# Attention, two feed-forward layers and a layer norm on one core: the ordering model lets VectorE and GpSimd take turns in SBUF, and gets new durations for the products

## The chip, the cores and the metric

One core of a Trainium2 chip runs the whole program as one launch. The metric is the device time of one execution in microseconds (us), the median of several. TensorE (PE) multiplies, VectorE (DVE), ScalarE (ACT) and GpSimd (POOL) do the elementwise work, SyncE (SP) issues the transfers.

## The reference

`x` is the output of an attention whose keys and values are averaged over 8 positions; two feed-forward layers of width 2048 follow, the first with a low-rank mixing over the sequence, the second behind a layer norm. All arrays are fp32.

```python
k_p = k.reshape(B, H, Sp, pool, D).mean(axis=3)        # B 8, H 8, S 576, D 64, pool 8, Sp 72
v_p = v.reshape(B, H, Sp, pool, D).mean(axis=3)
scores = scale * np.matmul(q, k_p.transpose(0, 1, 3, 2))
attn = softmax(scores)
x = np.matmul(attn, v_p)                               # then [8, 576, 512]
u = x + (x.transpose(0, 2, 1) @ U @ V).transpose(0, 2, 1)      # rank 32
x = u + np.maximum(u @ w_ch1, 0.0) @ w_ch2                     # 512 -> 2048 -> 512
xn = (x - mean) / np.sqrt(var + 1e-06) * g_ln
out = x + np.maximum(xn @ w2_ch1, 0.0) @ w2_ch2                # 512 -> 2048 -> 512
```

## The kernel before, in words

Products keep fp32 accuracy by splitting each operand into a high and a low fp32r part (`split`: a rounded copy, then a subtraction) and multiplying high by high, high by low and low by high. The weights of the feed-forward layers come as 64-bit words and are decoded with integer operations on VectorE (`decode`).

**First phase** (`phase_a`, up to about 665 us): for each of 8 batches the attention (`att_prep` averages the keys, `att_prep_v` the values, `att_m` does the softmax, `att_vm` the low-rank mixing), and one batch later the first 8 of the 16 hidden blocks of the first layer (`a_l1`, `a_l2`) out of resident weights. Before the first batch can go through `a_l1`, its 16 half blocks of weights have to be decoded and split.

**Three passes** (`passes`): the 4608 rows stand in 9 groups of 512. Pass 0 does the other 8 hidden blocks of the first layer, passes 1 and 2 the second layer. A group of a pass has 4 units, a unit 2 hidden blocks; 108 units in all. In a unit (`unit`) the first product is done with seven 2x2-block products (p1 to p7) of 6 matmuls with 256 columns each, into the PSUM tiles `pa` and `pbc`; VectorE adds pieces (lines 1301 and 1307), ScalarE takes the relu and VectorE its low part (line 1271). The second product (`second`, line 1331) is done a unit later in 8 pieces of three matmuls with 512 columns, into four PSUM tiles `py`. At a group's end VectorE adds the four `py` to `res` (`finish`, line 1346), which frees them for the next group.

While pass 0 does group g, the layer norm of group g-1 runs beside it (`norm`), in two halves of 256 rows: sum over the channels (lines 1412 to 1414), its high and low part `lnh` and `lnl`, a pair of matmuls with `ones` for the mean (lines 1404 and 1405), subtraction (1428), squares and their sum (1436 to 1440), the pair of matmuls again for the variance, a reciprocal on VectorE (1452) with a refinement (1454 to 1460), and four scalings of `res` (1467). Also beside it run `group_prep` (loading the next group, three differences of blocks at line 1198, and seven splits into `op` tiles, lines 369, 371 and 494), `residual` (line 1383), and, near the change of a pass, `load_pair` (the next weights, line 1163 and splits).

**The order is made by a planner.** Each operation is recorded by `Order.op` with its possible engines, a cost for each, and its tiles. `Order.schedule` then plays the program through a model: engines, costs, ring slots, semaphore delays. At each step an engine takes the available operation with the lowest `prio`, unless `better` says that another engine would end it sooner. Which engine an operation goes to and the order on each engine come out of this model alone; on the chip each engine then runs its list in order and waits only for data.

In the model before, VectorE and GpSimd never hinder each other. A product with n columns costs max(107, n / 2.4 + 2) ns: 108.7 for 256, 215.3 for 512. `prio` is the running sum of these costs at the point where the operation was recorded, plus a bias. GpSimd's cost of a 512-element line is 1227 ns (`c_pool`), VectorE's 601 (`c_dve`) or 335 (`c_fast`, for copies and scalar operations).

Of the kernel before, what the change touches and what calls it, by code (L numbers as in the profile page):

```python
# [16 lines left out]
PSUM = bass.MemoryType.PSUM  # L17
# [28 lines left out]

class Ring:


# [32 lines left out]


class Op:
    __slots__ = ("engs", "fn", "preds", "succs", "bufs", "prio", "ready", "wait", "eng", "start", "end", "alloc", "size")


PE, ACT, DVE, GP, SY = "pe", "act", "dve", "pool", "sync"  # L90
# [10 lines left out]
class Order:  # L101
# [3 lines left out]
    def op(self, engs, fn, r=(), w=(), prio=None, size=0):  # L105
        o = Op()
        o.engs, o.fn, o.succs, o.size = engs, fn, [], size
        o.prio = (self.clk + self.bias) if prio is None else prio
        o.eng = o.end = o.start = None
        preds, bufs = set(), []  # L110
        for wr, lst in ((False, r), (True, w)):
            for x in lst:
                b, k = x if isinstance(x, tuple) else (x, None)
                if b not in bufs:
                    bufs.append(b)
                for k2, (lw, rd) in b.acc.items():
                    if k is None or k2 is None or k == k2:
                        if lw is not None:
                            preds.add(lw)
                        if wr:  # L120
                            preds.update(rd)
        for wr, lst in ((False, r), (True, w)):
            for x in lst:
                b, k = x if isinstance(x, tuple) else (x, None)
                if wr:
                    if k is None:
                        b.acc = {None: (o, [])}
                    else:
                        b.acc[k] = (o, [])
                else:  # L130
                    lw, rd = b.acc.get(k, (None, []))
                    b.acc[k] = (lw, rd + [o])
        preds.discard(o)
        o.preds = len(preds)
        for p in preds:
            p.succs.append(o)
        o.bufs = [b for b in bufs if b.ring is not None]
        for b in o.bufs:
            b.left += 1
            b.ring.pool.left += 1  # L140
        o.ready = {e: 0.0 for e in engs}
        self.ops.append(o)
        if PE in engs:
            self.clk += engs[PE]
        return o


    def schedule(self):
# [5 lines left out]
        look = {e: never for e in engines}  # L154
        events, parked, order = [], {}, []
        dma, n, left, warm = 0.0, 0, len(self.ops), 0.0

        def at(e, t):
            if t < look[e]:
                look[e] = t  # L160
                heapq.heappush(events, (t, e))
# [8 lines left out]
        def blocked(o, t):  # L170

            for b in o.bufs:
                if b.slot is None:
                    r = b.ring
                    for a in r.pool.after:
                        if a.left:
                            return a
                        if a.end > t:
                            return a.end
                    if r.fifo and b.seq != r.turn:  # L180
                        return r, b.seq
                    if not r.free:
                        return r, None
                    if r.free[0][0] > t:
                        return r.free[0][0]
            return None
# [18 lines left out]
        while left:  # L205
# [4 lines left out]
            t, e = heapq.heappop(events)  # L210
# [7 lines left out]
            while fut and fut[0][0] <= t:  # L218
                _, k, o = heapq.heappop(fut)
                if o.eng is None:  # L220
                    heapq.heappush(av, (o.prio, k, o))
            got, later = None, []
            while av:
                pr, k, o = heapq.heappop(av)
                if o.eng is not None:
                    continue
                if any(x != e and better(o, x, t, t + o.engs[e] - (EAGER if e == GP else 0)) for x in o.engs):
                    later.append((pr, k, o))
                    continue
                why = blocked(o, t)  # L230
                if why is None:
                    got = o
                    break
                if isinstance(why, float):
                    heapq.heappush(fut, (why, k, o))
                else:
                    parked.setdefault(why, []).append(o)
# [8 lines left out]
            o, idle = got, 0  # L246
# [5 lines left out]
            o.eng, o.start = e, t  # L252
            free[e] = t + cost
            o.end = free[e]
            if e == SY:
                dma = max(dma, t + 1300) + o.size / RATE
                o.end = dma + 1000
# [88 lines left out]


def c_pe(n, k=1):
    return k * max(107.0, n / 2.4 + 2)


class View:
# [21 lines left out]
class Kern:  # L374
# [754 lines left out]
    def load_pair(self, p, j):  # L1129
# [30 lines left out]
        def comb(dst, i, key, a, b, op, extra=()):  # L1160
            o.op(
                {GP: c_pool(256), DVE: c_dve(256)},
                lambda e: getattr(e, op)(dst.t[:, i * 256 : i * 256 + 256], a(), b()),
                r=[x, *extra],
                w=[(dst, i)],
            )
# [426 lines left out]
```

## Time and profile before

| | |
|---|---|
| median of three timed runs | 1886.73 us (1885.02 to 1887.83) |
| profiled execution | 1894.99 us, span 1893.2 us |
| PE busy | 1798.2 us, 95% of the span |
| DVE busy | 1343.4 us, 71% |
| ACT busy | 691.3 us, 37% |
| POOL busy | 649.4 us, 34% |
| mean granted TensorE clock | 0.976 |

The span runs from the first to the last instruction; the profiled execution has 1.8 us around it. Busy shares are means over stages that differ, so the stages have to be read one by one. A granted clock of 1.0 is 2.4 GHz, of 0.5 it is 1.2 GHz; a value in between is the mean over a stretch. A matmul's records overlap with the next one's, so a stretch in which PE is fully busy can still run at the slower clock.

### The profile page before, as it was taken

To read this page: it belongs to the slowest core of one execution; us is meant where nothing else is said; L and a number is where in the kernel's file an instruction comes from. 1 tells how busy PE (TensorE), PEld (TensorE's weight loads), DVE (VectorE), ACT (ScalarE), POOL (GpSimd) and SP (SyncE) were. 2 spreads that over 40 slices of the span, in tenths; PEclk is the share of its full clock that TensorE was granted. 3 is DMA by queue.
4 is the path that set the end of the run, shared out by engine and by line. 5 is a ranking of instruction groups with operands and counts; after the bars stand their busy time and mean duration, and the time that the engine had idled before them with its cause. 6 is when DMAs were issued, how large, how long until landed. Compare 5 with 4: busy or idle time off the path is not lost. (4 is left out here: it accounts for less than half of the span.)

```text
span 1893.2 us, 30247 instructions
## 1 busy us (share of the span) xinstructions
PE 1798.2 (95%) x11482; PEld 1631.2 (86%) x11482; DVE 1343.4 (71%) x2414; ACT 691.3 (37%) x1965; POOL 649.4 (34%) x656
## 2 busy tenths in 40 slices
PE   5789999999999989999999989999999999999999
PEld 4578999999999988888787868888889898999888
DVE  8998888988854677988888898667543764444543
ACT  4445555555554223323333343323222322222221
POOL 5563444444301244443444664111111442111210
PEclk9699999999999999999999999999999999999999
DMA  5534454444312251323333332433211342222211
GB/s 167 157 116 148 127 159 151 140 139 158 107 55 81 88 188 60 124 99 112 112 112 112 111 119 93 140 128 112 79 47 65 129 153 109 93 109 89 89 68 45
DMA packets 88642, 212.42 MB, mean 112 GB/s; under 512 B 9264, under 2 KB 17456, under 8 KB 82736
## 3 DMA queue, kind: packets, MB, share of 16 engines
q1 hardware_dynamic: 88352, 210.49, 33.7%
q8 instruction: 90, 1.47, 0.3%
q14 instruction: 56, 0.46, 0.1%
q10 hardware_dynamic: 144, 0.00, 0.0%
HBM read 141.25 MB, written 69.21 MB: 111 GB/s over the span
## 5 line engine op out<-in xcount | busy, mean ns | idle before, releaser
L1331 PE MATMUL py<-hid,w2h 128*128 128x512 f32 x1728 | 552.2, 401 | 11.6 <-DVE res L1346 10.5
L1243 PE MATMUL pa<-op,w1h 128*128 128x256 f32 x1728 | 334.3, 286 | 17.8 <-DVE pa L1307 11.7
L1243 PEld LDWEIGHTS pa<-op,w1h 128*128 128x128 f32 x1728 | 296.8, 193 | 59.2 <-DVE pa L1307 18.6
L1331 PE MATMUL py<-hid,w2l 128*128 128x512 f32 x864 | 339.8, 393 | 0.0
L1331 PEld LDWEIGHTS py<-hid,w2h 128*128 128x128 f32 x1728 | 282.7, 193 | 27.7 <-DVE res L1346 8.4
L1243 PE MATMUL pbc<-op,w1h 128*128 128x256 f32 x1296 | 248.0, 284 | 3.3 <-DVE hid L1271 3.3
L1243 PEld LDWEIGHTS pbc<-op,w1h 128*128 128x128 f32 x1296 | 222.3, 191 | 29.8 <-DVE hid L1271 3.5
L1243 PE MATMUL pa<-op,w1l 128*128 128x256 f32 x864 | 246.8, 286 | 0.0
L1013 PE MATMUL pa<-hid,wh 128*128 128x288 f32 x1024 | 216.8, 304 | 10.1 <-DVE op L1025 9.7
L1046 PE MATMUL pbc<-op,wh 128*128 128x288 f32 x1024 | 215.5, 302 | 1.0 <-DVE wh L371 1.0
L1301 DVE TENSOR_TENSOR pbc<-s,pbc 128x512 f32<-128x512 f32 x108 | 74.6, 691 | 189.2 <-PE pbc L1243 185.9
L1331 PEld LDWEIGHTS py<-hid,w2l 128*128 128x128 f32 x864 | 164.8, 191 | 37.2
L1243 PE MATMUL pbc<-op,w1l 128*128 128x256 f32 x648 | 184.3, 284 | 0.0
L1013 PEld LDWEIGHTS pa<-hid,wh 128*128 128x128 f32 x1024 | 164.4, 190 | 16.6 <-DVE op L1025 15.4
L1046 PEld LDWEIGHTS pbc<-op,wh 128*128 128x128 f32 x1024 | 163.8, 188 | 5.9 <-issue 2.8
L1243 PEld LDWEIGHTS pa<-op,w1l 128*128 128x128 f32 x864 | 166.4, 193 | 0.0
L1265 ACT ACTIVATE hid<-pbc 128x512 fp32r<-128x512 f32 x108 | 64.6, 598 | 273.4 <-DVE pbc L1301 273.2
L1046 PE MATMUL pbc<-op,wl 128*128 128x288 f32 x512 | 151.5, 296 | 1.4 <-DVE wl L494 1.4
L1013 PE MATMUL pa<-hid,wl 128*128 128x288 f32 x512 | 151.4, 296 | 0.0
L369 ACT COPY s<-pa 128x256 f32<-128x256 f32 x204 | 75.7, 372 | 169.9 <-PE pa L1243 165.2
L494 POOL TENSOR_TENSOR op<-t,op 128x512 fp32r<-128x512 f32 x32 | 44.6, 1393 | 256.8 <-DVE op L371 250.9
L1265 ACT ACTIVATE hid<-pa 128x512 fp32r<-128x512 f32 x108 | 64.6, 598 | 168.2 <-PE pa L1243 159.3
(191 smaller groups left out, 3370.6 us busy)
## 6 DMA issues: line engine op xcount, KB each, us to landing
xraw<-n_d SPq DMA_DIRECT2D x18, 1024.0 KB, 4.8
wraw<-wC SPq DMA_DIRECT2D x32, 512.0 KB, 3.8
wraw<-wA SPq DMA_DIRECT2D x24, 512.0 KB, 3.8
w_d<-wx SPq DMA_DIRECT2D x48, 256.0 KB, 4.0
wraw<-w_d SPq DMA_DIRECT2D x48, 256.0 KB, 3.9
k<-kT SPq DMA_DIRECT2D x32, 288.0 KB, 2.9
q<-qT SPq DMA_DIRECT2D x32, 288.0 KB, 3.0
v<-v SPq DMA_DIRECT2D x32, 288.0 KB
```

Of the source, the lines that this page charges most:

```text
L369: e.copy(dst, src)
L494: lambda e: e.tensor_sub(lo(), src(), hi().bitcast(F32)),
L1013: e.matmul(ps.t[:, :SH], w.t[:, c], u, start=(i == 0), stop=(i == 3 * NCC - 1))
L1046: e.matmul(ps.t[:, :SH], w.t[:, c], x, start=(f == 0 and j == 0), stop=(f == NA - 1 and j == 2))
L1243: e.matmul(bank.t[:, sl], w.t[:, self.WCOL[k], c], u.t[:, t], start=(first and i == 0), stop=(last and i == 5), skip_group_check=True,)
L1265: lambda e: e.activation(h.t[:, :TG], bank.t, AF.Relu),
L1301: o.op({DVE: c_dve(TG)}, lambda e: e.tensor_add(c.t, s.t, c.t), r=[s], w=[c])
L1331: e.matmul(y.t, w.t[:, i, c], x.t[:, :TG], start=(first and q == 0), stop=(last and q == 2))
```

## The change

The model gets a port that VectorE and GpSimd share. An operation none of whose tiles lies in PSUM is marked `port`. While one of the two engines runs such an operation in the model, the other may not start one; it notes what it asked for (`asked`), goes on to operations that don't need the port, and the engine that has had the port leaves it to the other's operation where that has the lower `prio`. Nothing is enforced on the chip: no wait is added, and the turns exist only in the model that makes the order. The mark takes in every operation of VectorE without a PSUM tile, reductions and reciprocals too.

The second edit sets a product with n columns to n / 2.3 + 5 ns: 116.3 for 256, 227.6 for 512. With it all `prio` grow by some 6 to 7%, while the biases stay.

```diff
-    __slots__ = (..., "alloc", "size")
+    __slots__ = (..., "alloc", "size", "port")
...
+        o.port = not any(b.ring.pool.space is PSUM for b in o.bufs)
...
+        port, other, asked = {DVE: 0.0, GP: 0.0}, {DVE: GP, GP: DVE}, {}
...
             got, later = None, []
+            asked.pop(e, None)
...
                 why = blocked(o, t)
+                if why is None and e in port and o.port:
+                    z = asked.get(other[e])
+                    if port[other[e]] > t:
+                        why = port[other[e]]
+                        asked.setdefault(e, o)
+                    elif z is not None and z.eng is None and z.prio < o.prio:
+                        why = t + 1.0
...
+            if e in port and o.port:
+                port[e] = o.end
...
-    return k * max(107.0, n / 2.4 + 2)
+    return k * max(107.0, n / 2.3 + 5)
```

In the whole program GpSimd's list falls from 658 to 448 instructions, VectorE's grows from 2416 to 2514 and ScalarE's from 1648 to 1730; TensorE's 11292 and SyncE's 544 are the same in number. The lines of the changed kernel are 14 higher in this part of the file (line 1467 before is 1481 now).

**GpSimd, pass 0, a middle group, from the refinement of the first half's reciprocal on** (`op` are split inputs of the next group, `lns`, `lnq`, `lnv`, `lnd`, `res` belong to the norm, `t` and `xraw` to the preparation of the next group). Before:

```order
L1454 TENSOR_TENSOR lnv_6965<-lnv_6965,lnd_6966 128x256 x2
L494 TENSOR_TENSOR op_190<-xraw_6366,op_189 128x512
L1412 TENSOR_TENSOR lns_6962<-res_6957 128x256
L494 TENSOR_TENSOR op_192<-t_6368,op_191 128x512
L494 TENSOR_TENSOR op_194<-xraw_6366,op_193 128x512
L494 TENSOR_TENSOR op_196<-xraw_6366,op_195 128x512
L494 TENSOR_TENSOR op_198<-t_6367,op_197 128x512
L1428 TENSOR_TENSOR res_6957<-res_6957,lnm_6964 128x256
L1440 TENSOR_TENSOR lns_6962<-lns_6962,lnq_6963 128x256 x2
L1198 TENSOR_TENSOR t_6367<-xraw_6366 128x512
L494 TENSOR_TENSOR op_186<-xraw_6366,op_185 128x512
L1460 TENSOR_TENSOR lnd_6966<-lnd_6966,lnv_6965 128x256
```

The same place now:

```order
L1468 TENSOR_TENSOR lnv_6936<-lnv_6936,lnd_6937 128x256
L1474 TENSOR_TENSOR lnd_6937<-lnd_6937,lnv_6936 128x256
L1428 TENSOR_TENSOR lns_6933<-lns_6933,lnq_6934 128x256
L508 TENSOR_TENSOR op_184<-t_6337,op_183 128x512
L508 TENSOR_TENSOR op_186<-xraw_6336,op_185 128x512
L1212 TENSOR_TENSOR t_6337<-xraw_6336 128x512
L508 TENSOR_TENSOR op_188<-xraw_6336,op_187 128x512
L1212 TENSOR_TENSOR xraw_6336<-xraw_6336 128x2x256
L1426 TENSOR_TENSOR lns_6933<-res_6929 128x256
L1427 TENSOR_TENSOR lnq_6934<-res_6929 128x256
```

GpSimd now does three splits per group where it did six, and none of them stands between the refinement and the sum of the second half (line 1428, was 1414), which takes the `lnq` that VectorE makes behind its four scalings.

**VectorE, pass 0, the same place: the four scalings of the first half and what follows up to the second half's `lnl`.** Before:

```order
L1467 SCALAR_TENSOR_TENSOR res_6957<-res_6957,g_sb,lnd_6966 128x256 x4
L1271 SCALAR_TENSOR_TENSOR hid_202<-pa_231,hid_201 128x512
L1413 TENSOR_TENSOR lnq_6963<-res_6957 128x256
L371 COPY s_6954<-pa_232 128x256
L1414 TENSOR_TENSOR lns_6962<-lns_6962,lnq_6963 128x256
L371 CAST lnh_6960<-lns_6962 128x256
L371 CAST op_191<-xraw_6366 128x512
L494 TENSOR_TENSOR lnl_6961<-lns_6962,lnh_6960 128x256
```

Now:

```order
L1481 SCALAR_TENSOR_TENSOR res_6929<-res_6929,g_sb,lnd_6937 128x256 x4
L1426 TENSOR_TENSOR lns_6933<-res_6929 128x256
L1427 TENSOR_TENSOR lnq_6934<-res_6929 128x256
L1285 SCALAR_TENSOR_TENSOR hid_202<-pa_231,hid_201 128x512
L508 TENSOR_TENSOR op_188<-xraw_6336,op_187 128x512
L385 CAST op_189<-t_6338 128x512
L508 TENSOR_TENSOR lnl_6932<-lns_6933,lnh_6931 128x256
```

The two channel sums follow the scalings at once; their total is now GpSimd's and its high part ScalarE's; a split of an `op` and a cast stand ahead of `lnl`.

**TensorE, pass 0, the last unit of a middle group: the mean of the second half.** Before:

```order
L1331 MATMUL py_238<-hid_199,w2h_6363 128x512
L1331 MATMUL py_238<-hid_200,w2h_6363 128x512
L1331 MATMUL py_238<-hid_199,w2l_6365 128x512
L1243 MATMUL pbc_234<-op_193,w1h_6949 128x256
L1243 MATMUL pbc_234<-op_194,w1h_6949 128x256
L1243 MATMUL pbc_234<-op_193,w1l_6951 128x256
L1243 MATMUL pbc_234<-op_193,w1h_6949 128x256
L1243 MATMUL pbc_234<-op_194,w1h_6949 128x256
L1243 MATMUL pbc_234<-op_193,w1l_6951 128x256
L1404 MATMUL pbc_233<-lnh_6960,ones 128x256
L1405 MATMUL pbc_233<-lnl_6961,ones 128x256
```

Now:

```order
L1345 MATMUL py_238<-hid_199,w2h_6333 128x512
L1345 MATMUL py_238<-hid_200,w2h_6333 128x512
L1345 MATMUL py_238<-hid_199,w2l_6335 128x512
L1257 MATMUL pa_232<-op_189,w1h_6920 128x256
L1257 MATMUL pa_232<-op_190,w1h_6920 128x256
L1257 MATMUL pa_232<-op_189,w1l_6922 128x256
L1257 MATMUL pa_232<-op_189,w1h_6920 128x256
L1257 MATMUL pa_232<-op_190,w1h_6920 128x256
L1257 MATMUL pa_232<-op_189,w1l_6922 128x256
L1418 MATMUL pbc_233<-lnh_6931,ones 128x256
L1419 MATMUL pbc_233<-lnl_6932,ones 128x256
```

The pair stood behind the unit's fifth block product (p3, into `pbc`) and four pieces of the second product; it stands behind the third block product (p6, into `pa`) and two pieces now. The variance of the first half moves likewise in the unit before, from behind three block products and three pieces to behind two and one.

## Rows read from the trace of the kernel before

**Rows 1.** The page: busy time of the engines; TensorE's share and granted clock by slice

```profile
PE 1798.2 (95%) x11482; PEld 1631.2 (86%) x11482; DVE 1343.4 (71%) x2414; ACT 691.3 (37%) x1965; POOL 649.4 (34%) x656
PE   5789999999999989999999989999999999999999
PEclk9699999999999999999999999999999999999999
```

**Rows 2.** The chain that ended last, two neighbouring units of pass 2 (start, us, what)

```profile
1849.51 1.39 PE py L1331 x6
1850.90 0.71 PE pa L1243 x6
...
1860.05 1.39 PE py L1331 x6
```

**Rows 3.** Stretches: length, PE, PEld, DVE, ACT, POOL busy, clock, DMA, GB/s

```profile
0.00:135.70 135.70, 98.32 (x468) 79.93 (x468) 126.94 (x244) 62.05 (x254) 79.89 (x100) 0.86 0.49 146
135.70:665.30 529.60, 518.76 (x3818) 498.32 (x3817) 405.86 (x851) 265.58 (x933) 183.75 (x222) 1.00 0.39 123
...
709.90:1054.10 344.20, 322.33 (x1904) 284.81 (x1904) 283.74 (x453) 111.69 (x248) 146.70 (x139) 0.95 0.29 100
1054.10:1207.10 153.00, 138.33 (x812) 121.29 (x812) 129.99 (x209) 55.70 (x123) 77.50 (x67) 0.96 0.35 119
1207.10:1841.60 634.50, 633.49 (x3961) 568.92 (x3960) 346.28 (x585) 174.55 (x362) 142.03 (x113) 1.00 0.29 101
```

**Rows 4.** Who TensorE waited for in one group of pass 0, 1003 to 1055 us

```profile
PE py L1331 <- DVE res L1346: 1.9, 1, 1.9
PE pbc L1404 <- DVE lnh L371: 1.7, 1, 1.7
```

**Rows 5.** VectorE's timeline in pass 0 (start, length in us, what)

```profile
889.00 1.67 DVE L1467 SCALAR_TENSOR_TENSOR res<-res,g_sb,lnd 128x256 f32<-128x256 f32 x4
...
1040.07 5.29 DVE L1467 SCALAR_TENSOR_TENSOR res<-res,g_sb,lnd 128x256 f32<-128x256 f32 x4
...
1058.99 1.75 DVE L1452 RECIPROCAL lnd<-lnd 128x256 f32<-128x256 f32 x1 [0.54 <-ACT lnd L1447]
...
1064.99 4.64 DVE L1467 SCALAR_TENSOR_TENSOR res<-res,g_sb,lnd 128x256 f32<-128x256 f32 x4
1069.55 1.27 DVE L1346 TENSOR_TENSOR res<-res,py 128x512 f32<-128x512 f32 x2
```

**Rows 6.** GpSimd's timeline at the same places

```profile
1042.17 1.48 POOL L494 TENSOR_TENSOR op<-t,op 128x512 fp32r<-128x512 f32 x1
1043.61 1.47 POOL L494 TENSOR_TENSOR op<-xraw,op 128x512 fp32r<-128x512 f32 x1
...
1058.98 1.30 POOL L1198 TENSOR_TENSOR t<-xraw 128x512 f32<-128x512 f32 x1 [3.01 <-DMA xraw<-n_d]
...
1066.45 1.47 POOL L1198 TENSOR_TENSOR t<-xraw 128x512 f32<-128x512 f32 x1
```

**Rows 7.** Groups by line and shape: count, busy us, mean ns, idle before

```profile
L1467 DVE SCALAR_TENSOR_TENSOR res<-res,g_sb,lnd 128x256 f32<-128x256 f32 x72 | 66.5, 982 | 0.7 <-POOL lnd L1460 0.5
L733 POOL TENSOR_TENSOR v<-v 72x512 f32<-72x512 f32 x20 | 28.6, 1431 | 46.7 <-DMA v<-v 32.8 <-DVE xl L494 8.4 <-DVE wt L560 5.3
L733 POOL TENSOR_TENSOR v<-v 72x256 f32<-72x256 f32 x30 | 27.9, 930 | 14.7 <-DVE v L733 13.2
L707 POOL TENSOR_TENSOR k<-k 128x288 f32<-128x288 f32 x25 | 22.6, 904 | 2.9 <-DMA k<-kT 2.3
L707 POOL TENSOR_TENSOR k<-k 128x144 f32<-128x144 f32 x25 | 14.8, 591 | 2.0
L733 DVE TENSOR_TENSOR v<-v 72x512 f32<-72x512 f32 x12 | 8.3, 691 | 1.6 <-DMA v<-v 1.6
L708 POOL TENSOR_TENSOR kp<-k 128x72 f32<-128x72 f32 x25 | 12.3, 490 | 8.6 <-DVE kbd L371 6.9
L704 DVE TENSOR_REDUCE kp<-k 128x72 f32<-128x576 f32 x7 | 5.2, 749 | 3.9 <-DMA k<-kT 3.7
```

**Rows 8.** The line of the reciprocal: duration ns min/median/max, first and last start

```profile
L1452 DVE RECIPROCAL lnd<-lnd x18: 1740/1747/1754, 736.6 to 1169.4; 128x256 f32<-128x256 f32 x18
```

More of the change, by code (lines that the diff above doesn't have):

```diff
@@ L86 @@
 class Op:
-    __slots__ = ("engs", "fn", "preds", "succs", "bufs", "prio", "ready", "wait", "eng", "start", "end", "alloc", "size")
+    __slots__ = ("engs", "fn", "preds", "succs", "bufs", "prio", "ready", "wait", "eng", "start", "end", "alloc", "size", "port")
 PE, ACT, DVE, GP, SY = "pe", "act", "dve", "pool", "sync"
```

## The prediction

> **What bounds the kernel now.** I read the page first: TensorE is busy for 95% of the span, and the slices show it below nine tenths in the first three, the 15th and the 24th, with a low clock in the second [rows 1]. The chain that ended last then gives the floor: in pass 2 one unit follows the other after 10.54 us, made of pieces of 0.71 us for six matmuls with 256 columns and 1.39 us for six with 512, with nothing between [rows 2]. So a group of four units costs 42.16 us, and in pass 0 four pairs of statistics come on top, eight matmuls at 0.118 us (0.71 / 6), 0.95 us: 43.1 us.
>
> The busy time by stretch shows where time can be won [rows 3]. Behind 1207 us TensorE is idle for 1.0 us in 634: nothing to win. From 136 to 665 us it is idle for 10.8 of 529.6. What is left are three stretches. **Start**, 0 to 135.7 us, where VectorE is busy for 126.9 us, so VectorE is the bound. **Groups 1 to 7 of pass 0**, 709.9 to 1054.1 us: 344.2 us where 7 x 43.1 = 302 would do; of the 42 us too many, 21.9 are idle TensorE (344.2 - 322.3), about 17 are the granted clock (0.95, so 5% of the stretch lost at 1.2 GHz), 3 are small change. **The switch to pass 1**, 1054.1 to 1207.1 us, twelve units: 153.0 us where 12 x 10.54 + 2 = 128.5 would do.
>
> For the second stretch the waits name two places per group, and both hang on VectorE: 1.9 us for the freeing of `py` (line 1346) and 1.7 us for `lnh` of the second half's mean [rows 4]. VectorE's timeline shows why it is late. Ahead of both stand four scalings. Alone they take 1.67 us for all four (at 889.00); at 1040.07 they take 5.29 and at 1064.99 they take 4.64, and the freeing of `py` at 1069.55 is directly behind [rows 5]. At these times GpSimd runs one operation behind the other, 1.47 and 1.48 us each [rows 6]: a VectorE operation with both inputs in SBUF starts and then ends with GpSimd's. The two losses, 3.6 and 3.0 us, are larger than the waits of 1.7 and 1.9 us that come of them.
>
> **The change, part by part.** *The turns, at these two places.* In the new order GpSimd has, between the first half's refinement and the sum of the second half, nothing else, and that sum waits for VectorE's `lnq` behind the scalings. So GpSimd stands still during the first four: 5.29 falls to about 1.67, 3.6 us won. Behind them the way to `lnl` loses a relu part and a copy (0.68 and 0.41) and gains a split and a cast (0.69 and 0.42, estimates from the clean 256- and 512-wide operations), and a sum on GpSimd in place of VectorE, some 0.4 us longer. So `lnl` comes about 3.1 us sooner, counted from the reciprocal. The reciprocal itself can start 2.1 us sooner, since the variance is asked for two pieces and one product earlier (2 x 0.695 + 0.71). The mean is asked for two products and two pieces sooner, 2.8 us. The wait of 1.7 us becomes 1.7 - 3.1 - 2.1 + 2.8 = -0.7, none, with half a microsecond kept for collisions elsewhere. At the second four, GpSimd's load of the next group (`t`, `op`, `xraw`) is no longer held up by other work: it started at 1058.98 before [rows 6], three operations of 1.3 us then end near 1063, and the next one waits for VectorE's additions to `res`. So the second four are free as well, and `py` comes up to 3 us sooner: the wait of 1.9 us goes.
>
> *What it costs in VectorE's time there.* A middle group has 68 VectorE instructions where it had 66. They are the heavier ones, splits and residual additions: with the short durations of each form their sum is 38.5 us against 34.8, and GpSimd's falls from about 20 to 13. Records of neighbours overlap by some 0.08 us (1064.99 + 4.64 is 1069.63, the next starts at 1069.55 [rows 5]), so 33 us against 29.5 of VectorE's time. It is busy for 283.7 / 7 = 40.5 us per group now [rows 3], so 11 us are collisions, 6.6 of them at the two places. With those gone and a third of GpSimd's work away I take 4: 37 us in a group of 43.1. It fits, without much room: I keep about 1 us of waits per group for operations on PSUM that come late, and 0.8 for what remains of slow clock. 44.9 x 7 = 314, **-30 us** (bounds: -42 if TensorE never waits; +20, see the rivals).
>
> *The start.* Up to the 16th hidden part of the first batch VectorE gets 37 more instructions, 281 for 244: seven key reductions (0.749 each [rows 7]), twelve additions of values (0.69 for the wide ones), two softmax scalings and the like, 20.7 us undisturbed, 18 after the overlap. GpSimd loses seven key trios (0.904 + 0.591 + 0.490 = 1.99 us each), six value additions of 1.43 and six of 0.93, and some ten others, 43 us in all. What comes back: VectorE's 244 instructions there would take 107 us undisturbed, 88 without the overlap, and are busy for 126.9 beside 79.9 us of GpSimd [rows 3], so each microsecond of GpSimd stretches VectorE by 0.5; at 1040, where it runs without a pause, by 0.7 (3.6 of 5.3). So 21 to 30 us come back for 18 to 21 spent. With 0.5, which is of this stretch itself, it is -3 to 0; I take **0** (bounds -12 with 0.7, +18 if nothing comes back).
>
> Here a rule tells against the change. The reciprocal takes 1740 to 1754 ns in all its 18 places, with GpSimd running beside it (1058.98) or not [rows 5, 6, 8]: it needs no turn, but in the model it takes one. The Trainium skill, "SBUF — State Buffer", section "Who interferes with whom", says so in general: a VectorE instruction with at most one SBUF input, outside the two-port modes, does not contend with GpSimd, and a reduction never does on trn2; the trace agrees for the reciprocal. By it, the model's turns for 18 reciprocals and 22 reductions are wasted, 48 us (18 x 1.747 + 22 x 0.749) in which GpSimd is kept idle; an estimate from that page is that the start would get 3 to 4 us longer than I take it, and by the rows alone it stays at 0.
>
> *The switch to pass 1.* VectorE gets 24 more instructions in these twelve units (233 for 209), 15 us undisturbed, GpSimd loses about 35, some 38 us. At 0.5 it is 19 us back for 13 to 15: **-4** (bounds -14 and +13).
>
> *The new product times.* 0.71 / 6 = 118 and 1.39 / 6 = 232 ns are the trace's [rows 2], and the model now has 116 and 228. TensorE's list holds the same products. Passes 1 and 2 are at the floor, whatever their order: 0. The batches between 136 and 665 us have 10.8 us of idle TensorE to give and VectorE slack (405.9 of 529.6 busy [rows 3]), into which some 17 us of moved work fit: 0.
>
> Sum: -30 + 0 - 4 = -34 on the profiled 1894.99, 1861. The median of the timed runs is 8.3 us lower, so I predict **1853 us**.
>
> **The rivals.** *All of it goes* (0.13): pass 0 at its floor (-42), and start and switch at their better bounds (-26) would give 1819. For it: every loss named above is a collision. Against it: no wait enforces the turns.
>
> *The statistics are asked for before they are there* (0.12; slower). Three of four pairs stand 1.4 to 2.8 us earlier in TensorE's list, and a pair that waits holds up everything behind it. If the shortening doesn't come, since GpSimd runs when its data come and not when the model says, the second mean waits for 1.7 + 2.8 = 4.5 us and the others for up to 1.4 and 2.1: the 49.2 us per group (344.2 / 7) become some 52, +20 us, 1907. It decides where the four scalings still take over 4 us.
>
> *VectorE can't hold the moved work* (0.08; slower). Start and switch are where it is full. If a removed microsecond of GpSimd gives back less than 0.42 (18 / 43), the start gets longer; with 0.1 it is +14 and +9, and with half of pass 0's gain 1887 + 23 - 15 = 1895.
>
> *The change does nothing* (0.07): the turns are in the model alone, collisions move to other operations, and new waits take the place of the two: 1887.
>
> **How the numbers follow.** Forecast 0.60, the rivals as given. A measurement tells this kernel from no change at about 0.2%, 3.8 us. The range reaches from 1822, close to where all goes, to 1895, which takes in no change and the milder slower cases. Faster: 0.60 + 0.13 = 0.73. Same: 0.07. Slower: 0.20.
>
> **What would show it.** In the changed profile the groups of pass 0 should follow each other after 44 to 46 us; the four scalings (line 1481) should take about 0.47 us each, not 0.98 in the mean [rows 7]; the waits for `res` (1360) and `lnh` (1418) should be gone or under 0.5 us; GpSimd should be busy for some 440 us and VectorE for about as long as before; the 16th hidden part of the first batch should come between 126 and 144 us. Wrong I would be if a wait for `lnl` or for line 1321 of over 1.5 us stood in each group, or if the first phase ended over 10 us later.

## The result, and the profile after

The changed kernel takes 1838.71 us (median of four runs, 1836.65 to 1839.23); the kernel before took 1887.28 beside it (four runs, 1885.02 to 1892.27). The ratio is 0.9737, 95% interval 0.9716 to 0.9758. The gain of 48.6 us is inside the range forecast and larger than the 34 us that the sum gave, and its parts are not those of the sum. The profiled execution of the changed kernel took 1839.23 us, span 1837.4.

The page of the changed kernel, busy time of the engines, TensorE's share and granted clock by slice [for before, rows 1]:

```profile
PE 1769.2 (96%) x11482; PEld 1619.5 (88%) x11482; DVE 1279.1 (70%) x2512; ACT 723.4 (39%) x2047; POOL 435.6 (24%) x446
PE   5689999999999999999999999999999999999999
PEclk7689999999999999999999999999999999999999
```

GpSimd is busy for 214 us less. VectorE is busy for 64 us less, though it has 98 instructions more: its operations are stretched less. The two dips of TensorE's share behind the first three slices are gone.

The stretches of the changed kernel (start to the 16th hidden part; the rest of the first phase; groups 1 to 7 of pass 0; the switch; the rest), columns as in [rows 3]:

```profile
0.00:136.80 136.80, 96.52 (x464) 80.53 (x465) 118.15 (x281) 62.94 (x255) 43.12 (x53) 0.76 0.50 150
136.80:652.40 515.60, 514.16 (x3819) 497.04 (x3818) 395.07 (x879) 269.70 (x956) 127.60 (x157) 1.00 0.40 126
692.50:1018.50 326.00, 310.88 (x1903) 279.20 (x1902) 264.90 (x468) 122.79 (x278) 95.49 (x98) 0.97 0.32 107
1018.50:1153.50 135.00, 130.06 (x811) 116.57 (x811) 120.22 (x234) 58.30 (x129) 38.41 (x33) 1.00 0.40 135
1153.50:1837.40 683.90, 680.18 (x4249) 612.57 (x4247) 349.97 (x607) 195.73 (x405) 117.22 (x94) 1.00 0.28 96
```

All the kernels of this study cut at the same places of the program (the first VectorE instruction of the 16th hidden part of the first batch, then the first matmuls of units 0, 4, 32 and 44 of the passes, then the end), in us:

| kernel | start | to pass 0 | group 0 | groups 1 to 7 | switch | rest | span |
|---|---|---|---|---|---|---|---|
| before | 135.7 | 529.6 | 44.6 | 344.2 | 153.0 | 686.1 | 1893.2 |
| the change | 136.8 | 515.6 | 40.0 | 326.1 | 135.0 | 683.9 | 1837.4 |
| e1_turns_only | 133.1 | 515.3 | 41.8 | 305.9 | 133.0 | 685.6 | 1814.6 |
| e2_times_only | 137.5 | 533.9 | 40.4 | 333.0 | 162.5 | 694.1 | 1901.4 |
| e10_less_gpsimd | 136.6 | 518.1 | 40.1 | 332.7 | 155.3 | 685.5 | 1868.4 |
| e3_narrow_turns | 131.8 | 525.7 | 39.9 | 323.8 | 134.9 | 684.3 | 1840.5 |
| e5_rate | 148.4 | 523.5 | 43.9 | 306.0 | 135.5 | 696.0 | 1853.2 |
| e6_landing | 136.0 | 515.7 | 38.6 | 310.0 | 136.0 | 684.6 | 1820.9 |
| e7_fast_products | 136.1 | 510.4 | 42.6 | 302.4 | 141.7 | 683.9 | 1817.2 |
| e8_slow_products | 133.1 | 526.5 | 37.9 | 312.0 | 134.9 | 687.4 | 1831.8 |
| e9_turns_landing | 135.4 | 515.8 | 40.5 | 303.3 | 137.7 | 683.9 | 1816.6 |
| e11_fast_landing | 136.7 | 510.4 | 42.9 | 302.4 | 144.4 | 683.9 | 1820.6 |
| e12_faster_products | 133.1 | 514.1 | 49.6 | 301.2 | 142.5 | 683.8 | 1824.2 |

From before to the change, the first phase behind the start gave 14.0 us, group 0 4.6, groups 1 to 7 18.1 and the switch 18.0; the start lost 1.1 and the rest gave 2.2. That is 55.8 us between the two profiled spans.

In groups 1 to 7 the two waits of [rows 4] are gone. TensorE's waits there now, summed over the stretch (us in total, times, longest):

```profile
PE pa L1257 <- DVE pa L1321: 15.1, 7, 2.4
```

The line of the four scalings (L1481, before L1467 [rows 7]), duration in ns as minimum, median and maximum:

```profile
L1481 DVE SCALAR_TENSOR_TENSOR res<-res,g_sb,lnd x72: 467/478/1516, 722.5 to 1130.5; 128x256 f32<-128x256 f32 x72
```

Most of the scalings run undisturbed now, as forecast. But one wait stands in each of the seven groups: for the addition into `pa` at line 1321, 2.2 us in the mean (15.1 / 7), 1.4 in the first group and 2.2 to 2.4 in the others. It is the whole idle time of the stretch (326.0 - 310.88 = 15.1). It is not new. Before, TensorE's longest waits over the seven groups were these (line 1307 is line 1321 now):

```profile
PE py L1331 <- DVE res L1346: 8.8, 4, 2.9
PE pa L1243 <- DVE pa L1307: 6.9, 7, 2.6
PE pbc L1404 <- DVE lnh L371: 5.1, 3, 1.7
```

Two of the three are gone, and the third has doubled. VectorE's timeline in one group shows what is late:

```profile
927.74 1.75 DVE L1466 RECIPROCAL lnd<-lnd 128x256 f32<-128x256 f32 x1 [0.54 <-ACT lnd L1461]
929.52 2.86 DVE L1468 TENSOR_TENSOR lnv<-lnv,lnd 128x256 f32<-128x256 f32 x2
932.42 1.27 DVE L1471 TENSOR_SCALAR lnv<-lnv 128x256 f32<-128x256 f32 x1
933.73 0.43 DVE L1474 TENSOR_TENSOR lnd<-lnd,lnv 128x256 f32<-128x256 f32 x1
934.19 1.67 DVE L1481 SCALAR_TENSOR_TENSOR res<-res,g_sb,lnd 128x256 f32<-128x256 f32 x4
935.78 0.69 DVE L1315 TENSOR_TENSOR pbc<-s,pbc 128x512 f32<-128x512 f32 x1
936.37 0.68 DVE L1360 TENSOR_TENSOR res<-res,py 128x512 f32<-128x512 f32 x1
936.97 0.42 DVE L1321 TENSOR_TENSOR pa<-s,pa 128x256 f32<-128x256 f32 x1
```

and GpSimd's timeline at the same time:

```profile
929.38 1.29 POOL L1212 TENSOR_TENSOR t<-xraw 128x512 f32<-128x512 f32 x1 [5.47 <-DMA xraw<-u_d]
930.63 1.47 POOL L508 TENSOR_TENSOR op<-xraw,op 128x512 fp32r<-128x512 f32 x1
932.07 1.47 POOL L1212 TENSOR_TENSOR xraw<-xraw 128x512 f32<-128x512 f32 x1
```

The three operations that prepare the next group start when its load lands and run beside the refinement of the reciprocal (lines 1468 and 1471). The refinement takes 4.2 us (929.52 to 933.69), the scalings behind it are clean (1.67), and line 1321 starts 9.23 us behind the start of the reciprocal. It is so in six of the seven groups: the two operations of line 1468 take 2.7 to 2.9 us together there, and 0.88 where GpSimd stands still (at 720.42). The wait costs twice. The busy time and granted clock around it, in pieces of 4 us, and last the piece behind the wait two groups earlier:

```profile
930.00:934.00 4.00, 4.00 (x25) 3.53 (x24) 3.90 (x4) 0.00 (x0) 3.54 (x3) 1.00 0.01 4
934.00:938.00 4.00, 1.69 (x12) 1.40 (x12) 3.96 (x10) 0.86 (x2) 0.00 (x0) 1.00 0.36 147
938.00:942.00 4.00, 4.00 (x17) 3.46 (x16) 4.00 (x7) 1.38 (x3) 1.46 (x2) 0.57 1.04 348
942.00:946.00 4.00, 4.00 (x29) 3.69 (x28) 0.85 (x4) 0.75 (x2) 0.33 (x1) 1.00 0.93 283
...
844.00:848.00 4.00, 3.47 (x23) 3.20 (x24) 4.00 (x8) 1.42 (x4) 1.48 (x2) 1.00 1.01 378
```

After TensorE has stood for 2.3 us, the granted clock is 0.57 in the next 4 us, close to the lower level of 1.2 GHz, and then full again. Of the six waits of 2.2 us and more, five have such a piece behind them, at 0.57 to 0.67; behind the sixth, the one before 844 us, the clock stays at 1.00. Over the stretch it is 0.97. Of the 24 us that groups 1 to 7 lie above their floor of 302, 15.1 are the wait and some 9 the clock (0.97 of 326).

### The profile page after: what moved, and what is told of

Read it like the earlier page. It is cut to its first block, busy times and chain, and to the rows that moved or that the text cites. A ratio compares the mean times of both kernels' runs of the same rounds, so it can differ in the third digit from the quotient of the medians.

```text
span 1837.4 us, 30175 instructions
## 1 busy us (share of the span) xinstructions
PE 1769.2 (96%) x11482; PEld 1619.5 (88%) x11482; DVE 1279.1 (70%) x2512; ACT 723.4 (39%) x2047; POOL 435.6 (24%) x446
## 3 DMA queue, kind: packets, MB, share of 16 engines
q8 instruction: 90, 1.47, 0.3%
## 4 chain that ended last, share of the span: by engine, by line
PE 87%; DVE 9%; DMA 1%; ACT 1%; issue 1%; POOL 0%; SPq 0%; DVEq 0%; ACTq 0%; POOLq 0%
PE py L1345 30%; PE pa L1257 15%; PE pbc L1257 12%; PE pa L1027 11%; PE pbc L1060 10%; PE py L378 3%; PE py L767 2%; PE py L871 1%; DVE lnv L1468 1%; DVE res L1481 1%; DVE lnd L1466 1%; PE py L889 1%; PE py L890 1%; PE py L928 0%; DMA v<-v 0%
## 5 line engine op out<-in xcount | busy, mean ns | idle before, releaser
L1345 PE MATMUL py<-hid,w2h 128*128 128x512 f32 x1728 | 546.4, 398 | 0.0
L1257 PE MATMUL pa<-op,w1h 128*128 128x256 f32 x1728 | 328.5, 282 | 21.5 <-DVE pa L1321 19.8
L1345 PEld LDWEIGHTS py<-hid,w2h 128*128 128x128 f32 x1728 | 278.7, 191 | 13.4
L508 POOL TENSOR_TENSOR op<-t,op 128x512 fp32r<-128x512 f32 x26 | 35.2, 1356 | 393.0 <-DVE op L385 312.5
```

Of the source, the lines that this page charges most:

```text
L508: lambda e: e.tensor_sub(lo(), src(), hi().bitcast(F32)),
L1257: e.matmul(bank.t[:, sl], w.t[:, self.WCOL[k], c], u.t[:, t], start=(first and i == 0), stop=(last and i == 5), skip_group_check=True,)
L1345: e.matmul(y.t, w.t[:, i, c], x.t[:, :TG], start=(first and q == 0), stop=(last and q == 2))
```

## The experiments

Diffs are against the changed kernel where nothing else is said.

### The two edits apart

e1_turns_only keeps the turns and takes the old product times:

```diff
-    return k * max(107.0, n / 2.3 + 5)
+    return k * max(107.0, n / 2.4 + 2)
```

> The turns stay, a product costs n / 2.4 + 2 again in the model. If the turns are what counts, the four scalings take about 0.5 us each as in the changed kernel, GpSimd is busy for about 430 us, and the time is 1838 to 1855 us. If the new product times are what counts, the groups of pass 0 take 50 us again and the time is 1870 us or more. A share for each would stand between, 1855 to 1870.

e2_times_only keeps the new product times and marks nothing:

```diff
-        o.port = not any(b.ring.pool.space is PSUM for b in o.bufs)
+        o.port = False
```

> The new product times stay, no operation is marked for the port. If the turns are what counts, GpSimd is busy for about 600 us, scalings take about 1 us in the mean, the groups of pass 0 take 49 to 51 us and the time is 1875 to 1890 us. If the product times are what counts, it is 1838 to 1855 us. The first phase, which came out 13 us shorter than forecast, tells it by itself: its end (the first matmul of pass 0) at 650 to 655 us with the part that shortens it, at 660 to 668 without.

Turns alone: 1818.69 us, ratio 0.9626 [0.9606, 0.9645] to before. Times alone: 1904.25 us, 1.0069 [1.0053, 1.0085]. Both lie outside the times expected: 1838 to 1855 us for the turns alone, which gain more, and 1875 to 1890 for the times alone, which lose. Groups 1 to 7 and the switch with the turns alone, then the same with the times alone behind its stretch before pass 0:

```profile
690.10:996.00 305.90, 301.96 (x1899) 271.70 (x1898) 255.43 (x477) 118.59 (x267) 99.00 (x91) 1.00 0.31 111
996.00:1129.00 133.00, 131.69 (x816) 117.33 (x815) 123.94 (x239) 61.94 (x140) 34.98 (x33) 1.00 0.40 139
```

```profile
137.50:671.40 533.90, 521.81 (x3828) 500.56 (x3828) 394.17 (x855) 272.75 (x957) 187.31 (x225) 1.00 0.39 123
711.80:1044.80 333.00, 317.58 (x1905) 279.13 (x1904) 277.78 (x457) 113.80 (x257) 145.05 (x132) 0.97 0.30 103
1044.80:1207.30 162.50, 140.43 (x810) 123.08 (x809) 137.61 (x213) 54.43 (x119) 82.34 (x70) 0.94 0.34 117
```

All of the gain is the turns'; the product times take 1.1 percentage points of it away (0.9737 - 0.9626). Between the change and the turns alone, 20.2 of the 22.8 us of span lie in groups 1 to 7. The scalings take 602 ns in the mean with the turns alone, where about 0.5 us was expected and the change has 505, and its groups are shorter all the same: their mean does not tell the time by itself. The times by themselves leave VectorE nearly as stretched as before (277.8 us busy in groups 1 to 7, GpSimd 145.1). They win 11 us there and 4 in group 0, and lose more elsewhere: 1.8 at the start, 4.3 before pass 0, 9.5 at the switch and 8.0 behind it.

### Less GpSimd without turns

In the changed kernel GpSimd's list is a third shorter. So the gain could be less work on GpSimd, and not the turns as such. e10_less_gpsimd is the kernel before with one number of the model changed: GpSimd leaves an operation to another engine when that one would end it over 230 ns sooner, where it had to be over 1500 ns.

```diff
-EAGER = 1500.0
+EAGER = 230.0
```

> The kernel before, without turns and with its product times, in which GpSimd's head start over VectorE in the choice of an engine (EAGER) is 230 ns instead of 1500, so that GpSimd gets about as little work as with the turns (planned busy time 365 us; 384 with the turns and the same product times). If the gain comes of giving GpSimd less, whatever the order, the ratio is 0.960 to 0.970, like the turns alone with 0.963. If it comes of when the two use SBUF, part of it is missing: 0.973 to 1.000, with scalings of over 0.7 us in the mean and groups 1 to 7 at 320 us or more.

It took 1870.69 us, 0.9894 [0.9877, 0.9911]. GpSimd is busy for 444.9 us, close to the turns' 431.7. Its stretches from the 16th hidden part to pass 0, groups 1 to 7, and the switch, then TensorE's longest wait in groups 1 to 7:

```profile
136.60:654.70 518.10, 513.50 (x3812) 496.60 (x3811) 416.10 (x907) 266.42 (x938) 106.89 (x136) 1.00 0.39 125
694.80:1027.50 332.70, 313.67 (x1904) 278.45 (x1903) 275.36 (x455) 117.74 (x264) 125.78 (x125) 0.97 0.30 105
1027.50:1182.80 155.30, 137.77 (x811) 121.78 (x811) 137.77 (x220) 53.86 (x120) 65.59 (x60) 0.95 0.33 117
```

```profile
PE pa L1243 <- DVE pa L1307: 16.6, 10, 3.5
```

Its scalings (count, busy us, mean ns, idle before):

```profile
L1467 DVE SCALAR_TENSOR_TENSOR res<-res,g_sb,lnd 128x256 f32<-128x256 f32 x72 | 59.0, 876 | 0.7 <-POOL lnd L1460 0.6
```

The first phase gets most of its gain from less GpSimd alone (518.1 for the change's 515.6 and 529.6 before). Groups 1 to 7 get 11.5 us from it, where the change gets 18.1 and the turns alone 38.3: the scalings still take 876 ns in the mean, and TensorE waits for line 1307. The switch is no shorter than before. In the whole, 1.1 of the 3.7 points come with GpSimd's shorter list, and the other 2.7 only when the model also keeps the two engines apart in time. GpSimd's work isn't cut alike in every stretch by the two models (125.8 us for 99.0 in groups 1 to 7), so this split is a rough one.

### Turns for the operations that need none

Reciprocals took as long beside GpSimd as without it [rows 8], and so did the one key reduction that had it beside it before (0.74 us at 57.57, 0.74 to 0.75 in the other six). e3_narrow_turns lets them start, and lets GpSimd start beside them, without the port:

```diff
...
+        o.lone = lone
...
-                if why is None and e in port and o.port:
+                if why is None and e in port and o.port and not (e == DVE and o.lone):
...
-            if e in port and o.port:
+            if e in port and o.port and not (e == DVE and o.lone):
...
-                o.op({DVE: 1670}, lambda e: e.reciprocal(sd.t, sd.t), w=[sd])
+                o.op({DVE: 1670}, lambda e: e.reciprocal(sd.t, sd.t), w=[sd], lone=True)
```

and the same mark on the key reduction and the softmax's reciprocal.

> VectorE's reductions and reciprocals, which showed no stretching, take no turn in the model any more; everything else is as in the changed kernel. If turns that nothing needs cost time, GpSimd gets work back, its busy time rises by 10 us or more, and the time falls by 5 to 15 us. If they cost nothing, since VectorE's other work fills the place, it stays within 5 us of 1838.7.

1842.65 us, 0.9744 [0.9729, 0.9759]: the same as the change. GpSimd got work back (busy for 455.6 us, 20 more), but no time was won. The start is 5.0 us shorter, near the 3 to 4 that the prediction estimated for these turns, and the stretch behind it 10.1 longer. The Trainium skill, "SBUF — State Buffer", section "Who interferes with whom", says that a VectorE instruction with at most one SBUF input, outside the two-port modes, doesn't contend with GpSimd, and that a reduction never does on trn2. The trace agrees: in this kernel the two reciprocals that have GpSimd beside them for most of their time (at 1105.84 and 1126.39) take 1.74 and 1.75 us, as all 18 did before [rows 8], and the three key reductions that have it beside them take 0.73 to 0.75 us, as the other 15 do. That a wasted turn costs time in the whole no run shows.

### The load that lands sooner than the model says

The model lets a transfer land 1.3 us plus its bytes at 250 per ns plus 1.0 us behind its issue, 6.5 us for the 1 MB of a group. The page's row for such loads in passes 1 and 2 (KB each, us to landing) has 4.8. For those of pass 0, `xraw<-u_d`, which make the collision, it has no landing; the second line is the issue of the one in the group shown above.

```profile
xraw<-n_d SPq DMA_DIRECT2D x18, 1024.0 KB, 4.8
...
923.94 0.52 SPq L1222 DMA_DIRECT2D xraw<-u_d  x1
```

GpSimd takes this load up at 929.38, 5.4 us behind its issue, and 5.3 to 5.5 in the six groups with the collision. That is 1.0 to 1.2 us sooner than planned, and the 4.8 us of the two expectations below are sooner still. If the early landing makes the collision with the refinement, a model that knows the landing should remove it. e5_rate gives every transfer a faster rate, by which the group's load takes 4.8 us; e6_landing changes that one load alone.

```diff
-RATE = 250.0
+RATE = 420.0
```

> The model's transfers get 420 bytes per ns instead of 250, so that a load of 1 MB lands 4.8 us after its issue as in the trace, not 6.5. The theory: in the changed kernel GpSimd starts on the landed group 3.3 us sooner than the plan says, beside the refinement of the reciprocal (three VectorE operations stretched by 3.1 us), and TensorE then waits 2.3 us per group for line 1321. With the landing known, line 1321 is ahead of the scalings, the wait is under 0.7 us, groups of pass 0 take 43 to 45 us instead of 46.6, and the time is 1815 to 1828 us. The rival: VectorE is simply full in that unit; the wait stays at 1.5 us or more, or moves to another line, and the time is 1833 to 1845 us.

```diff
-            o.op({SY: 450}, lambda e: e.dma_start(x.t, src()), r=r, w=[x], size=4 * 262144)
+            o.op({SY: 450}, lambda e: e.dma_start(x.t, src()), r=r, w=[x], size=625000)
```

> The changed kernel, with one number other: only the load of a group (1 MB) is planned to land 4.8 us after its issue, as the trace shows it; all other transfers are planned as before. Up to the first such load the order is that of the changed kernel. The theory (the wait for line 1321 comes of GpSimd starting sooner on that load than planned): groups 1 to 7 take 304 to 312 us instead of 326, as with 420 bytes per ns for all (306), the start and the first phase stay at 652 us, and the ratio to the kernel before falls from 0.974 to 0.962 to 0.967. The rival (the gain with 420 came of something else in that plan): 320 to 328 us, ratio 0.972 to 0.976.

e5_rate: 1849.78 us, 0.9785 [0.9764, 0.9806], where 1815 to 1828 us was expected. Groups 1 to 7 are 20 us shorter than in the change, as expected, but the start is 11.6 longer, the stretch behind it 7.9 and the rest 12.1; the edit re-times every other transfer too. e6_landing: 1821.69 us, 0.9635 [0.9621, 0.965], and all but groups 1 to 7 is within 1.5 us of the change. Its groups 1 to 7, then TensorE's waits for line 1321 there, then VectorE behind the same reciprocal:

```profile
690.30:1000.20 309.90, 304.60 (x1904) 272.49 (x1903) 247.72 (x476) 121.26 (x271) 93.45 (x91) 1.00 0.31 110
```

```profile
PE pa L1257 <- DVE pa L1321: 2.1, 3, 1.4
```

```profile
915.60 1.74 DVE L1466 RECIPROCAL lnd<-lnd 128x256 f32<-128x256 f32 x1
917.25 0.63 DVE L1212 TENSOR_TENSOR t<-xraw 128x512 f32<-128x512 f32 x1
917.80 0.41 DVE L1468 TENSOR_TENSOR lnv<-lnv,lnd 128x256 f32<-128x256 f32 x1
918.13 0.68 DVE L1212 TENSOR_TENSOR xraw<-xraw 128x512 f32<-128x512 f32 x1
918.73 0.42 DVE L1468 TENSOR_TENSOR lnv<-lnv,lnd 128x256 f32<-128x256 f32 x1
919.07 0.69 DVE L1315 TENSOR_TENSOR pbc<-s,pbc 128x512 f32<-128x512 f32 x1
919.66 0.68 DVE L1360 TENSOR_TENSOR res<-res,py 128x512 f32<-128x512 f32 x1
920.26 0.42 DVE L1321 TENSOR_TENSOR pa<-s,pa 128x256 f32<-128x256 f32 x1
```

Now the model gives both operations of line 1212 to VectorE, between the two steps of the refinement, where they take 0.63 and 0.68 us. Line 1321 starts 4.66 us behind the start of the reciprocal, where it was 9.23. The wait falls from 15.1 to 2.1 us in the stretch, the clock is 1.00, and 16 us are won. So the collision makes the wait and the slow clock behind it in the changed kernel, and an earlier landing in the model is enough to take it away. That the landing alone puts it there is not shown. GpSimd starts on the load some 3.3 us sooner against the reciprocal than planned, and the transfer is only about 1.0 of that. In the plan that the changed kernel's model makes, GpSimd also waits 1.5 us for the turn of the four scalings, which nothing enforces on the chip, and the load is issued 3.0 us ahead of the reciprocal, where the trace has 3.8 (923.94 to 927.74). A plan with a landing of 5.4 us was not tried.

### How long the model should take a product to be

The measured durations made the order worse. Either durations nearer to the truth take a slack away that the old, short ones left, and then longer ones are worse still; or 2.3 has an unlucky collision. Three more values (with 2.55 and 2.7 the bound of 107 ns holds for 256 columns, so the 13% and 18% of the expectations are those of 512 columns; at 256 both are 9% below the trace):

```diff
-    return k * max(107.0, n / 2.3 + 5)
+    return k * max(107.0, n / 2.55 + 2)
```

> The turns, with products planned at n / 2.55 + 2 ns, shorter than in the kernel before and 13% below the trace. If a plan in which TensorE is too fast helps, because all that VectorE and GpSimd must deliver then has slack on the chip, groups 1 to 7 stay near the floor of 302 us (303 to 310) and the ratio is 0.957 to 0.967. If 2.4 was only a lucky place, it is anywhere, 0.965 to 0.985, with groups 1 to 7 at 315 us or more.

```diff
-    return k * max(107.0, n / 2.3 + 5)
+    return k * max(107.0, n / 2.15 + 5)
```

> The turns, with products planned at n / 2.15 + 5 ns, 5 to 6% above the trace. If slack is what counts, this has none: groups 1 to 7 take 328 us or more and the ratio is 0.975 to 0.995. If it is luck, the time has no relation to the product time and groups 1 to 7 may well be below 315 us.

```diff
-    return k * max(107.0, n / 2.3 + 5)
+    return k * max(107.0, n / 2.7 + 2)
```

> Turns, with products planned at n / 2.7 + 2 ns, 18% below the trace. If a plan with a fast TensorE gives slack, the first phase ends at 642 to 648 us (646.5 with 2.55, 648.4 with 2.4, 652.4 with 2.3, 659.6 with 2.15) and groups 1 to 7 stay at 302 to 308. If the order gets too far from what the chip does, the first phase ends later than 650 us or the groups take 312 us or more.

| model | time, us | ratio to before | first matmul of pass 0 | groups 1 to 7 |
|---|---|---|---|---|
| n / 2.7 + 2 (e12) | 1825.47 | 0.9658 [0.9643, 0.9672] | 647.2 | 301.2 |
| n / 2.55 + 2 (e7) | 1817.80 | 0.9614 [0.9598, 0.963] | 646.5 | 302.4 |
| n / 2.4 + 2 (e1) | 1818.69 | 0.9626 [0.9606, 0.9645] | 648.4 | 305.9 |
| n / 2.3 + 5 (the change) | 1838.71 | 0.9737 [0.9716, 0.9758] | 652.4 | 326.1 |
| n / 2.15 + 5 (e8) | 1832.76 | 0.9691 [0.9673, 0.971] | 659.6 | 312.0 |

Both hold in part. From 2.55 on to longer products the first phase ends later with each step, and with 2.55 and 2.7 TensorE stands for at most half a microsecond in groups 1 to 7. But that longer products are always worse fell: at 2.15 groups 1 to 7 are 14 us shorter than at 2.3. Groups 1 to 7 at 2.15:

```profile
697.50:1009.50 312.00, 304.97 (x1906) 272.34 (x1905) 257.12 (x490) 120.64 (x271) 85.94 (x83) 1.00 0.31 109
```

The wait for line 1321 is 6.8 us in six times, the longest 1.6, and the clock stays at 1.00. At 2.3 it is 2.2 us per group in the mean and the clock falls with it. The refinement's operations on VectorE (line 1468) take 940 ns in the mean at 2.3 and 457 to 502 in the other four. So among these five values the collision with the landing load is 2.3's own, and there is a smaller loss besides that grows with the length of the products in the model. At 2.7 another stretch pays, group 0. TensorE stands for 7.2 us of it, at a clock of 0.90:

```profile
647.20:696.80 49.60, 42.44 (x243) 37.63 (x242) 35.08 (x64) 12.39 (x26) 8.47 (x8) 0.90 0.58 200
```

### Both mends together

e9_turns_landing is e6_landing with n / 2.4 + 2, e11_fast_landing with n / 2.55 + 2.

```diff
-    return k * max(107.0, n / 2.3 + 5)
+    return k * max(107.0, n / 2.4 + 2)
...
-            o.op({SY: 450}, lambda e: e.dma_start(x.t, src()), r=r, w=[x], size=4 * 262144)
+            o.op({SY: 450}, lambda e: e.dma_start(x.t, src()), r=r, w=[x], size=625000)
```

> The turns with the old product times (ratio 0.963 alone) and the group's load planned to land after 4.8 us. There groups 1 to 7 already take 305.9 us, 4 above the floor. If the landing matters only where the plan leaves no slack, the ratio stays at 0.960 to 0.966; if it helps by itself, it falls to 0.955 to 0.960.

> Turns, products planned at n / 2.55 + 2 ns, and the group's load planned to land after 4.8 us. Groups 1 to 7 were at 302.4 us with the first two and are at their floor, so nothing is left for the landing there: 0.958 to 0.965. What can move is the switch to pass 1, which took 141.7 us there and 135 to 138 in the others; if the landing brings it to 136, the ratio is 0.958 to 0.961.

1818.66 us, 0.9617 [0.9602, 0.9633], and 1821.61 us, 0.9629 [0.9609, 0.965]. Neither is better, beyond the intervals, than the short products without the landing (0.9626 and 0.9614): groups 1 to 7 are at 303.3 and 302.4 us, where the floor is 302, so nothing is left there to win, and the second has a switch of 144.4. The best of the study are e7_fast_products and e9_turns_landing, some 72 to 73 us below the kernel before (1817.80 x (1 / 0.9614 - 1) = 73.0) and 1.2 points below the change; the intervals part them neither from each other nor from e1, e6 and e11.

## Why the prediction was right, and where its steps failed

**The mechanism in pass 0 was right.** Four scalings next to a GpSimd that runs without a pause were what delayed VectorE. They went from 982 ns in the mean [rows 7] to 505, the waits for `res` and `lnh` went, and GpSimd's busy time came out at 435.6 us where some 440 was forecast. VectorE, forecast to be busy for about as long as before, came out 64 us lower. The working has a relu part leave the way to `lnl`; it still stands ahead of it on VectorE (at 914.04, `lnl` at 916.11), without a wait. The turns alone brought groups 1 to 7 to 305.9 us, between the 302 of the better bound and the 314 of the forecast.

**The term of -30 us for groups 1 to 7 came out at -18.** The step that failed is "three operations of 1.3 us then end near 1063": they were timed against the scalings alone, and these are clean indeed. The refinement ahead of the scalings was left out of the working, and two of its operations have two SBUF inputs too. The three operations fall on it and stretch it to 4.2 us; that gives the wait for line 1321 of 2.2 us per group, which the prediction named as the sign that it would be wrong. The trace of before already had both. In the group at 855 us the refinement stood beside the work on a landed load (VectorE, then GpSimd):

```profile
856.92 1.86 DVE L1454 TENSOR_TENSOR lnv<-lnv,lnd 128x256 f32<-128x256 f32 x2
858.82 1.26 DVE L1457 TENSOR_SCALAR lnv<-lnv 128x256 f32<-128x256 f32 x1
...
857.12 1.38 POOL L1198 TENSOR_TENSOR t<-xraw 128x512 f32<-128x512 f32 x1 [5.55 <-DMA xraw<-u_d]
```

And the waits were read from one group [rows 4], whose pair stands in the last three of the seven only; the 6.9 us for line 1307 over all seven were left out. The 44 to 46 us per group became 46.6 (326.1 / 7). e6_landing, which changes only the planned landing of these loads, gives 16 of the us back.

**"The new product times: 0" failed.** The argument was that the list of TensorE's products is the same and that passes 1 and 2 are at their floor. That holds for those passes (within 4 us of the change's 683.9 in all kernels but e2_times_only and e5_rate). It forgot that the times also set when VectorE and GpSimd are planned to work in pass 0. Alone the times cost 0.69%, beside the turns 1.1 points; with other values in the same place the gain is as large as 3.9%.

**"The batches between 136 and 665 us: 0" failed** for the sign of 14 us. They had 10.8 us of idle TensorE to give [rows 3], and 9.4 of these were won: TensorE now stands for 1.4 us in that stretch (515.60 - 514.16). The other 4.6 are busy time of TensorE (518.76 to 514.16). The working called VectorE's slack large enough to take the moved work and looked no further; that the same slack could end the idle time was left out. Less GpSimd does most of it, as e10_less_gpsimd shows with 518.1 us.

**The switch, -4 forecast, came out at -18**, 4 beyond the bound of -14. The mechanism was right and the size off: a removed microsecond of GpSimd was taken to give back half a microsecond of VectorE, so that the 24 moved instructions would eat most of it. VectorE is now busy for 120.2 us with 234 instructions where it was for 130.0 with 209 [rows 3]. That is 9.8 us less where 4 to 6 were reckoned, for 39.1 us less of GpSimd: with the 13 to 15 us reckoned for the added ones, a rate of about 0.6. The granted clock, which the working left out there, went from 0.96 to 1.00, an estimated 6 us of the stretch (0.04 x 153). e10_less_gpsimd, with GpSimd at 65.6 us, won nothing there. That points to the meeting in time more than to the amount of work, but with 12 us less of GpSimd for the change's 39 it doesn't settle it.

**The start at 0 was right in its time, but not by its working.** It takes 136.8 us for 135.7. VectorE is busy for 118.2 us there, 8.8 less than before, with 281 instructions for 244. With the 18 us reckoned for the added ones, 27 came back for 36.8 us less of GpSimd (79.89 to 43.12), so the rate was 0.73, that of the better bound, and not 0.5. That VectorE's 8.8 us brought nothing is seen in what TensorE waits for in this stretch:

```profile
PE py L378 <- DVE sc L818: 13.1, 3, 9.9
PE pa L1027 <- DVE op L1039: 8.8, 3, 5.9
```

Two long waits for VectorE, the softmax's scaling and a hidden part, hold this stretch now; before, the longest were 12.8 us for the keys (`kbd`) and 7.3 for `gs`. What puts these two behind other work of VectorE there was not tried.

**The rivals.** That all of it goes (1819) is what the turns alone do, by another distribution: 1818.69. That the statistics are asked for too early didn't come, since the scalings ahead got short. That VectorE can't hold the moved work didn't come either. Of the last rival, that new waits take the place of the two, a part came: the wait for line 1321 grew from 6.9 to 15.1 us.

**What stays open:** which other step loses time as the model's products get longer (first matmul of pass 0 from 646.5 to 659.6 us), and why the switch is 142 to 144 us in e7, e11 and e12 and 133 to 138 in the others with turns. TensorE stands for 7.9 to 9.4 us of it in these three, at a clock of 0.96, and for 1.3 to 5.1 in the others, but for other lines in each: 6.4 us at once for the low part of a relu (line 1285) in e7, and several shorter waits in e11 and e12.

## What to carry to other kernels

A VectorE operation with both inputs in SBUF next to a GpSimd that runs without a pause can cost about three times its own duration (5.29 us for 1.67 before), so a plan that keeps the two apart in time is worth more than one that only gives GpSimd less (2.7 points beside 1.1 here). Turns in a plan without waits hold only as well as the plan's other times: look first at the transfer that releases the other engine, and set its landing from the profile of that very load. A truer number in a model can make its order worse, so a model with several numbers wants each of them tried alone.

## What the runs showed that was not expected

GpSimd also stretches an operation of VectorE with one SBUF input: line 1471, a scalar operation on `lnv`, took 1.27 us beside GpSimd's operation on `xraw` at 932.07, and 0.28 in the turns-only kernel at 898.13. GpSimd pays as well: its first operation, under way before the refinement began, took 1.29 us, the two behind it 1.47 each.

Of six waits of 2.2 to 2.4 us in the changed kernel, five left TensorE at a granted clock of 0.57 to 0.67 in the 4 us behind them and one at 1.00; over the stretch it is 0.97. Six waits of at most 1.6 us in the same groups of e8_slow_products left it at 1.00 over the stretch.
